# Four key heads of one batch per round: K and V each in one DMA of 128 rows, V's gradient first

## The chip, the core and the metric

The kernel runs on one core of a Trainium2 chip. The metric is the device time of one execution in microseconds (us). Three timed executions of the kernel before took 770.71, 771.0 and 772.86 us; the median, 771.0 us, is the time before. One further execution was profiled. It took 770.8 us, of which the profile's span covers 769.0 us. A core has five engines that run their own instruction streams: TensorE (PE), VectorE (DVE), ScalarE (ACT), GpSimd (POOL) and SyncE (SP). SP, ACT and POOL issue the DMAs, and every DMA runs on the same 16 DMA engines.

## What is computed

The kernel computes one decode step of a block and its gradients. A normalised input `xn` (2 batches, 512 features) goes through two branches: sliding-window attention against a cache, and a small dense layer with squared ReLU. The output is `x + s * silu(dense)`. The part that matters here is the attention branch and its gradients:

```
W = 4096                                   # the window: the last 4096 of 32768 positions
q = (xn @ wq) as 32 heads of 128           # 4 query heads share one of 8 key heads
p = softmax(q . k / sqrt(128))             # k, v: [2 batches, 8 heads, 4096, 128] of the window
o = p @ v ;  s = o @ wo
# gradients, for each batch and key head:
dv = p^T do                                # do: gradient that arrives at o
dp = do . v ;  ds = p * (dp - sum(dp * p))
dk = ds^T q ;  dq = ds k
```

The gradients of the K and V caches are returned whole: `out_2` and `out_3`, each [2, 8, 32768, 128] in bf16. Only the window of 4096 positions has values; the 28672 positions before it are zero in every head and have to be written.

## The kernel before, in words

**The zero fill.** Lines 91 to 114: POOL writes the zero positions of `out_2` and `out_3` from a tile of zeros `zt`, one head after the other, as 47 DMAs that are all issued from POOL's queue in order; each waits until an earlier one has landed, so that a limited number is under way. The very last head's zeros are written by SP at the end (line 626), after SP's store of `out_6`, and only when the second to last of POOL's fills has landed.

**The prologue** (lines 193 to 325). SP loads `w1`, `w2`, `wo` and `wq` (lines 203 to 207). Layer norm, the dense layer, `do` (lines 274 to 292) and `q` (294 to 304) are computed, and `w1` and `w2` are transposed for later (306 to 325). Its tiles live in a pool that is closed at its end, and the tiles `knat` and `vnat` for K and V are allocated after it in the same memory (lines 342 and 343), so the first loads of K and V wait for the prologue's end.

**A round** (lines 417 to 499) handles two key heads of both batches, that is four pairs of head and batch; there are four rounds. The window of one pair, 4096 x 128 bf16 values or 1 MB, is contiguous in memory; it is seen as 32 rows of 128 positions, 32 KB each. Pair number `pr` goes to the partitions `pr, pr+4, pr+8, ...` of a 128-partition tile by a DMA of 32 rows of its own (lines 345 to 347), so K of a round comes in four DMAs, and V too. Because of this interleaving the transposes use a permuted identity `pperm` (line 181), and `p_bf` and `ds_bf` are written with a stride of four elements (lines 440 and 452). The order inside a round is:

1. `scores(s_ps, knat, zq)` (lines 368 to 381): transpose K in 16 groups of eight blocks on PE, copy each group out of PSUM by DVE or ACT, multiply with the queries.
2. Softmax, and `p_bf` on ACT (line 440).
3. `scores(dp_ps, vnat, zdo)`, then `ds_bf` on DVE (line 452).
4. `contract(ds_bf, knat)` for dq (lines 383 to 399); then `outer_store` (401 to 412) makes the gradient of K: 32 matrix products (line 407), each evicted from PSUM by ACT or DVE into `knat` itself, and four DMAs of 1 MB from ACT's queue into `out_2` (line 412). Then SP loads K of the next round into `knat`, each quarter as soon as the store of that quarter has landed.
5. The same for V: `contract(p_bf, vnat)` for o, `outer_store` into `vnat`, four stores into `out_3`, four loads of the next V.
6. For the round's two heads the gradient of `wq` (lines 473 to 499), which overwrites `wq` in place.

The compiler's scheduler moves instructions of these steps past each other where their data allow it: the transposes of V, for instance, begin between those of K.

**The epilogue** (lines 501 to 633) takes tiles in the memory that `knat` and `vnat` give up, so it begins when the last stores have landed. It makes the output, the remaining gradients, the last zero fill on SP (626) and the store of `wo`'s gradient (633).

Of the kernel before, what the change touches and what calls it, by code (L numbers as in the profile page):

```python
# [16 lines left out]
def kernel(  # L17
# [36 lines left out]
    G = 8  # L54
    HH = 2
    NP = HH * B
    PB = P // NP
# [78 lines left out]
    doT_all = const.tile([P, HQ, B], BF16, name="doT_all")  # L136
    oT_all = const.tile([P, HQ, B], BF16, name="oT_all")
    dxqT = const.tile([P, DK, B], F32, name="dxqT")

# [40 lines left out]
    nc.vector.tensor_scalar(out=nsel[:], in0=sel[:], scalar1=1e30, scalar2=-1e30, op0=ALU.mult, op1=ALU.add)  # L180
    pperm = const.tile([P, NP, PB], BF16, name="pperm")
    nc.vector.tensor_copy(out=pperm[:], in_=ident_bf[:].rearrange("p (k b) -> p b k", b=NP))
    ZO = R - REP
# [3 lines left out]
    nc.vector.memset(zdo[:], 0.0)  # L187
    p_bf = const.tile([R, CC, PB, NP], BF16, name="p_bf")
    nc.vector.memset(p_bf[:], 0.0)
    ds_bf = const.tile([R, CC, PB, NP], BF16, name="ds_bf")  # L190
    nc.vector.memset(ds_bf[:], 0.0)

    with tc.tile_pool(name="pw", bufs=1) as pw:
# [7 lines left out]
        dma_store.dma_start(out=b2_bf[:], in_=B_b2.rearrange("(p k) -> p k", k=DK))  # L201
        w1 = pw.tile([P, DK, F], BF16, name="w1")
        dma_load.dma_start(out=w1[:], in_=B_w1.rearrange("(p k) f -> p k f", k=DK))
        w2 = pw.tile([P, FK, D], BF16, name="w2")
        dma_load.dma_start(out=w2[:], in_=B_w2.rearrange("(p j) d -> p j d", j=FK))
        dma_load.dma_start(out=wo[:], in_=A_wo.rearrange("(p j) m -> p j m", j=NJ))
        dma_load.dma_start(out=wq[:], in_=A_wq.rearrange("(p k) n -> p k n", k=DK))

        tp = ps_m.tile([P, DK, B], BF16, tag="m")
# [63 lines left out]

        do_rows = pw.tile([B, N], BF16, name="do_rows")
        JG = 4
# [17 lines left out]

        q_rows = pw.tile([B, N], BF16, name="q_rows")
        for n0 in range(0, N, 512):
# [30 lines left out]

    attn = ExitStack()
    kvp = attn.enter_context(tc.tile_pool(name="kvp", bufs=1))
    kvt = attn.enter_context(tc.tile_pool(name="kvt", bufs=3))
    wsl = attn.enter_context(tc.tile_pool(name="wsl", bufs=1))  # L330
    small = attn.enter_context(tc.tile_pool(name="small", bufs=1))
    one = attn.enter_context(tc.tile_pool(name="one", bufs=1))

    kwin = slice(SK - W, SK)

    def rows_of(t, b, h):
        return t[b, h, kwin, :].rearrange("(p c) d -> p c d", c=NCB)

    def pairs(r):
        return [(hh * B + b, b, r * HH + hh) for hh in range(HH) for b in range(B)]  # L340

    knat = kvp.tile([P, NCB, DH], BF16, name="knat")
    vnat = kvp.tile([P, NCB, DH], BF16, name="vnat")

    def load(src, r, nat):
        for pr, b, h in pairs(r):
            dma_load.dma_start(out=nat[pr:P:NP], in_=rows_of(src, b, h))

# [6 lines left out]
    def block_diag(hT):  # L355
        zr = small.tile([P, HH, B, G, REP], BF16, tag="zr")
        for hh in range(HH):
            for b in range(B):
                nc.vector.tensor_copy(out=zr[:, hh, b],
                                      in_=hT[:, hh * REP:(hh + 1) * REP, b].unsqueeze(1).to_broadcast([P, G, REP]))  # L360
        rp = ps_m.tile([R, P], F32, tag="m")
        nc.tensor.matmul(rp[:], lhsT=zr[:].rearrange("p h b g i -> p (h b g i)"), rhs=ident_bf[:, :], start=True, stop=True)
        bd = one.tile([R, G, DH], BF16, tag="bd")
        nc.vector.tensor_tensor(out=bd[:], in0=rp[:].unsqueeze(1).to_broadcast([R, G, DH]),  # L364
                                in1=m8[:].unsqueeze(2).to_broadcast([R, G, DH]), op=ALU.mult)
        return bd

    def scores(out_ps, nat, zbuf):
        n = 0
        for half in range(NH):  # L370
            for g in range(G):
                tp = ps_t.tile([P, CH, P], BF16, tag="pt")
                for j in range(CH):
                    nc.tensor.transpose(tp[:, j, :], nat[:, g * CC + half * CH + j, :], pperm[:].rearrange("p b k -> p (b k)"))  # L374
                tT = kvt.tile([P, CH, NP, PB], BF16, tag="tT")
                evac(tT[:].rearrange("p c b k -> p (c b k)"), tp[:].rearrange("p c k -> p (c k)"), eng=("act" if n % 4 == 3 else "dve"))
                n += 1
                for pr in range(NP):
                    o = ZO - (pr * RB + REP * g)
                    nc.tensor.matmul(out_ps[:, half * CH * PB:(half + 1) * CH * PB], lhsT=zbuf[:, pr, o:o + R], rhs=tT[:, :, pr, :],  # L380
                                     start=(g == 0 and pr == 0), stop=(g == G - 1 and pr == NP - 1))

    def contract(src, nat):
        cols = []
        for half in range(NH):
            tp = ps_t.tile([P, CH, R], BF16, tag="pt")
            for cc in range(CH):
                nc.tensor.transpose(tp[:, cc, :], src[:, half * CH + cc].rearrange("r k b -> r (k b)"), ident_bf[:, :])
            t = one.tile([P, CH, NP, G, REP], BF16, tag=f"colT{half}")
# [11 lines left out]
    def outer_store(src, bd, nat, dst, r):  # L401
        st = nat[:].rearrange("p (g c) d -> p g c d", g=G)
        n = 0
        for cc in range(CC):
            for gh in range(2):
                ov = ps_o.tile([P, 4, DH], F32, tag="o")
                nc.tensor.matmul(ov[:], lhsT=src[:, cc].rearrange("r k b -> r (k b)"), rhs=bd[:, gh * 4:(gh + 1) * 4, :],  # L407
                                 start=True, stop=True)
                evac(st[:, gh * 4:(gh + 1) * 4, cc, :], ov[:], eng=("act" if n % 8 in (0, 1, 3, 4, 6) else "dve"))
                n += 1  # L410
        for pr, b, h in pairs(r):
            dma_store.dma_start(out=rows_of(dst, b, h), in_=nat[pr:P:NP])

    NR = HKV // HH
    load(A_k_cache, 0, knat)
    load(A_v_cache, 0, vnat)
    for r in range(NR):
        hs = slice(r * HH * REP, (r + 1) * HH * REP)
        for hh in range(HH):
            hq = slice((r * HH + hh) * REP, (r * HH + hh + 1) * REP)  # L420
            nc.vector.tensor_copy(out=zq[:, hh * B:(hh + 1) * B, ZO:ZO + REP], in_=qT_all[:, hq, :].rearrange("p i b -> p b i"))
            nc.vector.tensor_copy(out=zdo[:, hh * B:(hh + 1) * B, ZO:ZO + REP], in_=doT_all[:, hq, :].rearrange("p i b -> p b i"))

        s_ps = ps_s.tile([R, CW], F32, tag="sd")
        scores(s_ps, knat, zq)
# [12 lines left out]
        for pr in range(NP):  # L438
            rb = slice(pr * RB, (pr + 1) * RB)
            nc.scalar.activation(out=p_bf[rb, :, :, pr], in_=e_sb[rb], func=ACT.Copy, scale=rl[rb, 0:1])  # L440

        dp_ps = ps_s.tile([R, CW], F32, tag="sd")
        scores(dp_ps, vnat, zdo)
        dpp = small.tile([R, 1], F32, tag="dpp")
# [5 lines left out]
        for pr in range(NP):  # L450
            rb = slice(pr * RB, (pr + 1) * RB)
            nc.vector.scalar_tensor_tensor(out=ds_bf[rb, :, :, pr], in0=dp_c[rb], scalar=delta[rb, 0:1], in1=p_bf[rb, :, :, pr],  # L452
                                           op0=ALU.subtract, op1=ALU.mult)

        dq_ps = contract(ds_bf, knat)
        dqT_bf = small.tile([P, HH, REP, B], BF16, tag="dqT_bf")
        for hh in range(HH):
            nc.scalar.mul(out=dqT_bf[:, hh].rearrange("p i b -> p b i"), in_=dq_ps[:, hh * B:(hh + 1) * B, :], mul=SCALE)
        bdq = block_diag(qT_all[:, hs, :])
        outer_store(ds_bf, bdq, knat, out_2, r)  # L460
        if r + 1 < NR:
            load(A_k_cache, r + 1, knat)

        o_ps = contract(p_bf, vnat)
        for hh in range(HH):
            hq = slice((r * HH + hh) * REP, (r * HH + hh + 1) * REP)
            nc.vector.tensor_copy(out=oT_all[:, hq, :].rearrange("p i b -> p b i"), in_=o_ps[:, hh * B:(hh + 1) * B, :])
        bddo = block_diag(doT_all[:, hs, :])
        outer_store(p_bf, bddo, vnat, out_3, r)
        if r + 1 < NR:  # L470
            load(A_v_cache, r + 1, vnat)

        for hh in range(HH):
            hk = r * HH + hh
            wqT = wsl.tile([P, REP, DK, P], BF16, tag="wqT")
# [8 lines left out]
            for k in range(DK):  # L484
                for i in range(REP):
                    nc.tensor.matmul(xps[:, k, :], lhsT=wqT[:, i, k, :], rhs=dqT_bf[:, hh, i, :], start=(i == 0), stop=(i == REP - 1))
            if hk == 0:
# [4 lines left out]
            for i in range(REP):  # L492
                nc.tensor.transpose(tp[:, i, :], dqT_bf[:, hh, i, :], ident_bf[:, :])
            dq_rows = small.tile([B, REP * DH], BF16, tag="dq_rows")
# [166 lines left out]
```

## Time and profile before

| What | Value |
|---|---|
| Median of three timed runs | 771.0 us |
| The profiled execution: time, span | 770.8 us, 769.0 us |
| Busy share of the span: PE, DVE, ACT, POOL | 53%, 36%, 28%, 4% |
| Bytes moved by DMA | 326.73 MB, mean 425 GB/s |
| of them read from and written to memory | 45.62 MB, 280.50 MB |
| One load of K or V: a DMA of 1024 KB, issue to landing | 14.8 us and 14.7 us (medians) |
| One store of 1024 KB, K and V | 28.0 us and 31.0 us (medians) |
| One zero fill of 7168 KB | 162.9 us (median, several under way) |

How to read it: the time of an execution is a little longer than the span, since the span runs from the first to the last recorded instruction. The profile's second part cuts the span into 40 slices of 19.2 us and gives, for each, the busy share of every engine in tenths, the clock granted to PE, the mean busy share of the 16 DMA engines and their bandwidth. The third part lists the DMA queues: q0 is POOL's, q1 SP's, q10 ACT's; its columns are the number of packets, the MB, and the time of the packets as a share of the time of all 16 DMA engines. The chain of waits follows the work that ended last back to its beginning; each of its lines is a start, a duration and what took it.

### The profile page before, as it was taken

How to read it: one execution, taken by the hardware profiler on the slowest of the kernel's cores; microseconds unless marked ns; L12 is line 12 of the kernel's file. 1: busy time of each engine (PE TensorE's matmuls, PEld its weight loads, DVE VectorE, ACT ScalarE, POOL GpSimd, SP SyncE). 2: the span in 40 equal slices, each digit the busy share in tenths (PEclk: the TensorE clock that was granted, in tenths of full speed). 3: DMA queues.
4: the chain of work that ended last, by engine and by line, in shares of the span. 5: the costliest groups of instructions: out<-in, count | busy, mean ns of one | idle time of the engine just before them, and what ended most of it. 6: DMA issues, size and time to landing. Idle time of an engine off the chain costs nothing.

```text
span 769.0 us, 9484 instructions
## 1 busy us (share of the span) xinstructions
PE 407.4 (53%) x4110; PEld 273.6 (36%) x4118; DVE 279.2 (36%) x496; ACT 213.9 (28%) x317; POOL 31.9 (4%) x55
## 2 busy tenths in 40 slices
PE   0166740875870656578034649702746784075690
PEld 0153330755520545442034447201635541034220
DVE  3033330435650232555012355610324463014770
ACT  0034430240660114066001315700231273010360
POOL 3000000010100000000000000000000000000000
PEclk9997895986975788688569687955978696565555
DMA  9999999999999999999999999999999999999988
GB/s 360 427 432 426 434 434 431 425 428 434 430 432 426 430 431 432 431 432 428 433 432 429 433 432 427 430 432 432 430 433 427 427 432 430 431 439 423 394 374 373
DMA packets 14971, 326.73 MB, mean 425 GB/s; under 512 B 3109, under 2 KB 3118, under 8 KB 3128
## 3 DMA queue, kind: packets, MB, share of 16 engines
q0 software_dynamic: 9728, 227.55, 70.1%
q1 hardware_dynamic: 3082, 56.63, 18.0%
q10 hardware_dynamic: 2120, 41.95, 12.9%
q8 instruction: 32, 0.52, 0.2%
q14 instruction: 9, 0.07, 0.0%
HBM read 45.62 MB, written 280.50 MB: 424 GB/s over the span
## 4 chain that ended last, share of the span: by engine, by line
DMA 41%; PE 31%; DVE 12%; ACT 9%; issue 4%; ACTq 1%; SPq 0%; DVEq 0%
DMA out_dram<-vnat 16%; DMA out_dram<-knat 13%; DMA vnat<-in_A_v_cache_dram 8%; PE dp_ps L380 5%; DMA b_bf<-in_B_b_dram 4%; PE ov L407 4%; PE tp L374 4%; PE ps L396 3%; DVE ds_bf L452 3%; ACT p_bf L440 2%; ACT tT L147 2%; PE wps L631 2%; DVE tT L149 2%; ACT knat L147 2%; PE dops L286 1%
## 5 line engine op out<-in xcount | busy, mean ns | idle before, releaser
L149 DVE COPY tT<-tp 128x1024 bf16<-128x1024 bf16 x96 | 64.3, 689 | 245.4 <-PE tp L374 245.4
L374 PE MATMUL tp<-pperm,knat 128*128 128x128 bf16 x512 | 42.2, 234 | 112.5 <-DMA knat<-in_A_k_cache_dram 85.6
L147 ACT COPY tT<-tp 128x1024 bf16<-128x1024 bf16 x32 | 32.4, 1012 | 181.3 <-PE tp L374 181.2
L374 PEld LDWEIGHTS <-knat 128*128 128x128 bf16 x512 | 37.0, 106 | 120.0 <-issue 118.3
L380 PE MATMUL dp_ps<-tT,zdo 128*128 128x256 bf16 x256 | 44.8, 314 | 31.1 <-ACT tT L147 24.1
L374 PE MATMUL tp<-pperm,vnat 128*128 128x128 bf16 x512 | 45.9, 246 | 25.8 <-DMA vnat<-in_A_v_cache_dram 23.4
L97 POOL DMA_DIRECT2D out_dram<-zt x47 | 30.8, 661 | 531.5 <-DMA out_dram<-zt 528.3
L407 PE MATMUL ov<-bd,p_bf 128*128 128x512 bf16 x124 | 44.3, 416 | 13.1 <-DVE bd L364 6.8
L374 PEld LDWEIGHTS <-vnat 128*128 128x128 bf16 x512 | 40.6, 113 | 29.3 <-issue 26.6
L147 ACT CAST knat<-ov 128x512 bf16<-128x512 f32 x80 | 43.9, 590 | 23.5 <-PE ov L407 20.2
L147 ACT CAST vnat<-ov 128x512 bf16<-128x512 f32 x80 | 43.5, 593 | 21.8 <-PE ov L407 10.7
L407 PE MATMUL ov<-bd,ds_bf 128*128 128x512 bf16 x124 | 45.5, 413 | 1.9 <-issue 0.9
L380 PE MATMUL s_ps<-tT,zq 128*128 128x256 bf16 x256 | 40.9, 293 | 10.4 <-DVE tT L149 6.2
L380 PEld LDWEIGHTS <-zdo 128*128 128x128 bf16 x256 | 27.5, 110 | 40.4 <-issue 35.2
L149 DVE CAST knat<-ov 128x512 bf16<-128x512 f32 x48 | 32.9, 691 | 23.5 <-PE ov L407 14.1
L149 DVE CAST vnat<-ov 128x512 bf16<-128x512 f32 x48 | 33.0, 692 | 21.9 <-PE ov L407 21.3
L380 PEld LDWEIGHTS <-zq 128*128 128x128 bf16 x256 | 25.8, 104 | 16.9 <-issue 13.6
L396 PEld LDWEIGHTS <-vnat 128*128 128x128 bf16 x512 | 20.1, 99 | 17.7 <-issue 12.2
L147 ACT CAST wq<-wps 128x512 bf16<-128x512 f32 x16 | 8.7, 591 | 59.0 <-DMA out_dram<-knat 54.9
L440 ACT ACTIVATE p_bf<-e_sb,rl 32x512 bf16<-32x512 f32 x16 | 22.8, 1428 | 6.7 <-DVE rl L437 6.5
L396 PE MATMUL ps<-t,vnat 128*128 128x16 bf16 x512 | 21.5, 171 | 5.9 <-issue 5.8
L407 PEld LDWEIGHTS <-p_bf 128*128 128x128 bf16 x128 | 12.0, 101 | 32.2 <-issue 28.3
(204 smaller groups left out, 526.8 us busy)
## 6 DMA issues: line engine op xcount, KB each, us to landing
out_dram<-zt POOLq DMA_DIRECT2D x26, 7168.0 KB, 162.9
knat<-in_A_k_cache_dram SPq DMA_DIRECT2D x16, 1024.0 KB, 14.8
vnat<-in_A_v_cache_dram SPq DMA_DIRECT2D x16, 1024.0 KB, 14.7
out_dram<-knat ACTq DMA_DIRECT2D x16, 1024.0 KB, 28.0
out_dram<-vnat ACTq DMA_DIRECT2D x16, 1024.0 KB, 31.0
out_dram<-zt POOLq DMA_DIRECT2D x4, 3584.0 KB, 56.6
out_dram<-zt SPq DMA_DIRECT2D x1, 7168.0 KB, 30.9
out_dram<-zt POOLq DMA_DIRECT2D x1, 5040.0 KB, 73.7
```

The lines of the kernel that those rows point to most:

```text
L97: sw_fill.append(nc.gpsimd.dma_start(out=v, in_=zs))
L147: nc.scalar.copy(out=out_ap, in_=in_ap)
L149: nc.vector.tensor_copy(out=out_ap, in_=in_ap)
L286: nc.tensor.matmul(dops[0:B, :, :], lhsT=dsT_bf[:, dk, :], rhs=woT[:, :, dk, :], start=(dk == 0), stop=(dk == DK - 1))
L374: nc.tensor.transpose(tp[:, j, :], nat[:, g * CC + half * CH + j, :], pperm[:].rearrange("p b k -> p (b k)"))
L380: nc.tensor.matmul(out_ps[:, half * CH * PB:(half + 1) * CH * PB], lhsT=zbuf[:, pr, o:o + R], rhs=tT[:, :, pr, :], start=(g == 0 and pr == ...
L396: nc.tensor.matmul(ps[:], lhsT=nat[:, g * CC + half * CH + cc, :], rhs=cols[half][:, cc, :, g, :], start=(half == 0 and g == 0 and cc == 0 ...
L407: nc.tensor.matmul(ov[:], lhsT=src[:, cc].rearrange("r k b -> r (k b)"), rhs=bd[:, gh * 4:(gh + 1) * 4, :], start=True, stop=True)
L440: nc.scalar.activation(out=p_bf[rb, :, :, pr], in_=e_sb[rb], func=ACT.Copy, scale=rl[rb, 0:1])
L452: nc.vector.scalar_tensor_tensor(out=ds_bf[rb, :, :, pr], in0=dp_c[rb], scalar=delta[rb, 0:1], in1=p_bf[rb, :, :, pr], op0=ALU.subtract, o ...
L631: nc.tensor.matmul(wps[:], lhsT=o_rows[:, j:N:NJ], rhs=ds_rows[:, :], start=True, stop=True)
```

## The change

A round now handles four key heads of one batch (the rounds are heads 0 to 3 of batch 0, then of batch 1, then heads 4 to 7 of each). The four heads' windows are 32 rows of 32 KB each, and one DMA carries all 128 rows, head `h` to the partitions `32h` to `32h+31`: one load per round for K and one for V, and one store for each. In memory a head's 32 rows are contiguous, and the next head begins 32768 positions further on, so the memory side of this DMA has the dimensions 4 heads x 32 rows x 16384 elements, and the tile's side 128 x 16384. With that layout the plain identity takes the place of `pperm`, and `p_bf` and `ds_bf` are written without a stride.

The order in a round changes: scores with V first, then scores with K, softmax, `p_bf`; then o and V's gradient, its store and the next V load; then dq and K's gradient, its store and the next K load. The first V is loaded in the prologue, behind `wq` in SP's queue, into memory of its own; `w1` and `w2` lie in K's tile, so K's first load still waits until they have been transposed. `do_rows` and `q_rows` share memory. dq is kept for both batches, and the gradient of `wq` is computed in the second round of each set of heads, for four heads at a time. The zero fill, its DMAs and its order are unchanged.

```diff
-    HH = 2
-    NP = HH * B
+    NP = 4
...
-    pperm = const.tile([P, NP, PB], BF16, name="pperm")
-    p_bf = const.tile([R, CC, PB, NP], BF16, name="p_bf")
+    p_bf = const.tile([R, CC, NP, PB], BF16, name="p_bf")
...
+    w12 = kvp.tile([P, NCB * DH], BF16, tag="k")
+    w1 = w12[:, 0:DK * F].rearrange("p (k f) -> p k f", k=DK)
+    w2 = w12[:, DK * F:DK * F + FK * D].rearrange("p (j d) -> p j d", j=FK)
+    rounds = [(b, h0) for h0 in range(0, HKV, NP) for b in range(B)]
+
+    def kv_of(t, r):
+        b, h0 = rounds[r]
+        return t[b, h0:h0 + NP, SK - W:SK, :].rearrange("h (k c) d -> h k (c d)", c=NCB)
+
+    def load(src, r, tag):
+        nat = kvp.tile([P, NCB * DH], BF16, tag=tag)
+        dma_load.dma_start(out=nat[:], in_=kv_of(src, r))
+        return nat[:].rearrange("p (c d) -> p c d", d=DH)
...
         dma_load.dma_start(out=wq[:], in_=A_wq.rearrange("(p k) n -> p k n", k=DK))
+        vnat = load(A_v_cache, 0, "v")
...
-    def load(src, r, nat):
-        for pr, b, h in pairs(r):
-            dma_load.dma_start(out=nat[pr:P:NP], in_=rows_of(src, b, h))
...
-        for pr, b, h in pairs(r):
-            dma_store.dma_start(out=rows_of(dst, b, h), in_=nat[pr:P:NP])
+        dma_store.dma_start(out=kv_of(dst, r), in_=nat.rearrange("p c d -> p (c d)"))
...
+    knat = load(A_k_cache, 0, "k")
     for r in range(NR):
...
+        dp_ps = ps_s.tile([R, CW], F32, tag="sd")
+        scores(dp_ps, vnat, zdo)
         s_ps = ps_s.tile([R, CW], F32, tag="sd")
         scores(s_ps, knat, zq)
...
+        bddo = block_diag(heads(doT_all, r))
+        o_ps = contract(p_bf, vnat)
...
+        outer_store(p_bf, bddo, vnat, out_3, r)
+        if r + 1 < NR:
+            vnat = load(A_v_cache, r + 1, "v")
+
+        bdq = block_diag(heads(qT_all, r))
         dq_ps = contract(ds_bf, knat)
...
         outer_store(ds_bf, bdq, knat, out_2, r)
         if r + 1 < NR:
-            load(A_k_cache, r + 1, knat)
...
+            knat = load(A_k_cache, r + 1, "k")
+
+        b, h0 = rounds[r]
+        for hk in range(h0, h0 + NP) if b == B - 1 else ():
```

## Prediction

> **What bounds the kernel now.** I read the slices first, for which resource is full; then the queue table, for what fills it; then the chain of waits in order of time, for what a round of K and V costs.
>
> The slices, their DMA rows:
>
> ```profile
> DMA  9999999999999999999999999999999999999988
> GB/s 360 427 432 426 434 434 431 425 428 434 430 432 426 430 431 432 431 432 428 433 432 429 433 432 427 430 432 432 430 433 427 427 432 430 431 439 423 394 374 373
> ```
>
> All 16 DMA engines are full from the first slice to the last. 326.73 MB at the middle's 431 GB/s are 758 us of the span's 769; the rest is the start and the end. The kernel is bound by bytes, and the change moves not one byte less. It can win only in the lulls, and lose by leaving engines idle.
>
> The queue table (packets, MB, share of 16 engines):
>
> ```profile
> q0 software_dynamic: 9728, 227.55, 70.1%
> q1 hardware_dynamic: 3082, 56.63, 18.0%
> q10 hardware_dynamic: 2120, 41.95, 12.9%
> ```
>
> Two readings. First, the speed of one engine: q10 moved 41.95 MB in 12.9% of 16 x 769.0 us = 1587 engine-us, so 26.4 GB/s per engine; q0 gives the same 26.4. Second, how many engines a DMA is dealt to. q10 carried 32 stores of 32 rows, two of 128 rows (`wq`, `wo`), two small loads of 128 rows and two of 2 rows: 1024+256+256+4 = 1540 rows. That leaves 580 packets: 16 for each of the 36 DMAs of 32 or 128 rows (576), and 2 for each of the two with 2 rows (4). q1 agrees: 2437 data packets, and 645 = 40 DMAs x 16, two 2-row DMAs x 2 and a 1-row DMA x 1. So each engine of a DMA leaves one small packet, and a DMA's first dimension decides the number of engines: 16 for 32 or 128 rows, two for 2 rows, one for 1.
>
> The chain of one round (start, us, what):
>
> ```profile
> 380.34 31.85 DMA out_dram<-vnat
> 412.20 12.36 DMA vnat<-in_A_v_cache_dram
> 424.69 1.01 PE tp L374 x8
> ...
> 485.47 33.10 DMA out_dram<-knat
> ```
>
> V arrives at 424.6, K's store goes out at 485, both stores and the last quarter of the V load take 77 us more, and V arrives again at 561.8: 137 us per round, hidden under the fill. The last fill follows at 735.0, behind the epilogue.
>
> **The DMA shape, on which all turns.** The new DMA's memory side has the dimensions 4 x 32 x 16384 (the heads are 32768 positions apart and cannot be merged with the rows), its tile side 128 x 16384. In the trace both sides of every DMA have the same first dimension, so it does not show which side rules. The rows bound it: 16 engines, if 128 rules, or 4, if the smaller does. I take 4: the pieces must be cut alike on both sides, and 16 shares of a first dimension of 4 do not exist, as they did not for 2 rows and for 1. That the four are the same ones each time I take too, and price the other case below.
>
> [...]
>
> **Part 1, the four engines' load.** K and V move 16 x 4.19 MB = 67.1 MB; on four engines that is 16.8 MB each. The fill puts 227.55/16 = 14.2 MB on each, the rest (326.73-227.55-67.1 = 32.1 MB) 2.0. Together 33.0 MB, at 26.4 GB/s **1250 us** for these four; the twelve others have 16.2 MB, 615 us. So even with no idle moment the span is 1250, as an end of the range.
>
> **Part 2, the chain on top of it.** One K or V transfer, alone on four engines: 4.19 MB / (4 x 26.4 GB/s) = 39.7 us. Beside others it gets these shares:
> - load beside fill, window 20 to 50: q1 54.9%, so 39.7/0.55 = 72 us
> - store beside fill, window 645 to 672: q10 46.0%, so 86 us
> - store, load and fill, window 385 to 410: 29.5%, 31.5%, 41.2%, so about 130 us for store and load together.
>
> First K arrival: `wq` landed at 57; V behind it takes 72 (129); K, which is issued at 108 when `w1` and `w2` are transposed, follows in SP's queue with another 72: **201**. V was there at 129, so its scores (20 us) are done.
>
> From K's arrival to V's store: scores with K 20 us (395.3 to 415.6 before, 15 of 16 groups), softmax and `p_bf` 10 (426.5 to 436.5), transposes of `p_bf` and contraction 7 (461.6 to 467, with DVE's copy), 32 products with their evictions 16 (468.9 to 485): **53 us**. Then V's store 86; under it `ds_bf` (5.4 us), the dq contraction (5.4) and K's product and evictions (16), 27 in all, are hidden. K's store, behind V's in ACT's queue, runs beside the next V load: 130. Then K's load, under which V's scores are hidden: 72. A round is 53+86+130+72 = **341 us**.
>
> How long the fill lasts on the four engines: it needs 14.2 MB/26.4 = 539 us of each. Until 201 it got about 85 (201, less 8 of start, less 29 for `w1`, `w2`, `wo`, `wq`, less 79 for V and K); each round gives it 341 - 4 x 39.7 = 182. So it has 267 at 542, 449 at 883, and ends in the third round, near 1006. From there transfers run undisturbed: in that round V's store ends at 1015, K's store and V's load share the engines (79, to 1094), K's load 39.7, to 1134. Last round: 53, V's store 39.7, K's store 39.7: 1266. The epilogue then takes what it took before, from 674.7 to 735.0, 60 us, and the last fill and `wo`'s store 34 (735.0 to 769.0): a span of **1360 us**, and with the 1.8 us around it 1361.8. The profiled execution (770.8) stands 0.2 us under the median, so I take 1362.
>
> **Smaller parts.**
> - 48 fewer issues and their packets: SP's four K issues took 2.45 us, ACT's four stores 2.41. All are beside full DMA engines; between windows with few and many small packets (275 to 340 and 245 to 275) the bandwidth differs by 431 to 426 GB/s. Zero taken, at most 1% of the K/V stretches gained.
> - The staged quarters go: SP's next load used to start after one quarter of the store (four issues spread over 21.9 us) and now waits for all of it. Behind it in SP's queue is only the next K load, which waits for a later store. Priced in the round above, which has no overlap of a store with its own load.
> - `p_bf` and `ds_bf` without stride: L440 took 1.43 us on ACT, L452 1.34 on DVE. Below, the nearest row is the 128x512 eviction, 0.59 (ACT) and 0.69 (DVE); above, no change. A gain of 0 to 3.4 us per round for `p_bf`; `ds_bf` hides under V's store. I take the nearest row, L440 itself, zero. That a stride gone makes it slower, I exclude: same elements, same engine. `ident_bf` for `pperm`: the same 128x128 product, zero.
> - PE's clock: granted 0.79 in the window 425 to 485; longer pauses might raise it, or not. If all 53 us shrank by 0.79, 11 us per round, 44 in all, to the lower side.
> - V in the prologue: a loss of DMA time to nobody, since the prologue waits for small loads of `b1`, which land before (33.7).
> - The gradient of `wq`, four heads in the last round where there were two: 16 evictions of 0.59 or 0.69 and 8 copies of `wqT` of 0.68 or 1.03 us, some 17 us, under K's last store of 39.7. Without that cover, 17 us more.
> - Shared memory of `do_rows` and `q_rows`: the transposes of `do_rows` ended at 90.0, the first `q_rows` products at 88.3; up to 1.7 us, hidden as K's load waits for V's.
>
> **The rivals.**
> 1. *Sixteen engines (128 rules)*, which ends on the other side. Place: the stores and loads. A transfer then takes a quarter: 18 us for a load, 21 for a store, 32 for both; a round 53+21+32+18 = 124 instead of 137, K arrives at 126, the last store ends at 126+372+53+21+10 = 582 instead of 674.7. For it: every 128-row DMA here ran on 16. Price: bytes stay the bound, so only the lull before the last fill closes (window 727 to 736: 2.27 MB where 431 GB/s give 3.88, 3.7 us): 767. It decides whenever the dealing gives 16 engines: then there is no loss to pay for. If the lull stays because the fill's last DMAs still end first, 771.
> 2. *Four engines, but different ones each time.* Against it, nothing in the trace. The engines' loads even out, the fill ends near 740; rounds cost 53+86+80+72 = 291 beside it (K's store and V's load apart) and 53+3 x 39.7 = 172 after it: 201+2 x 291+172+53+79+60+34, about 1181.
> 3. *Fill starved or favoured.* In the 4-engine case with other shares: a fill that gets less early leaves less idle later, down to 1250 and the start's 8, 1258; one that runs out a round earlier leaves them idle for 53 us more, 1415, and with the `wq` work uncovered 1432.
>
> **How the numbers follow.** Four fixed engines 0.79, four changing 0.06, sixteen 0.13 (0.09 at 767, 0.04 at 771), other 0.02, which I count as slower. The likeliest is 1362; its own range, 1258 to 1432, takes in clock, `p_bf` and shares. The other 4-engine case brings the lower end to 1180; that leaves out the sixteen and a little, 2 in 10. A measurement of this kernel can tell some 0.3% from no change. Faster 0.09, same 0.04, slower 0.87.
>
> **What would show it.** The small packets: with four engines q1 falls to 3082-512+32 = 2602 packets and q10 to 1640; with sixteen to 2698 and 1736. The DMA row drops to fives and sixes, about 240 GB/s; a 4096 KB load lands after 70 us or more instead of some 18; `ds_bf` and K's evictions end under V's store; DMA takes over half of the chain. What would make me wrong: q1 at 2698, and the DMA row still at nines.

## The result and the profile after

The changed kernel takes 1500.3 us (median of four runs, 1493.4 to 1501.7), against 770.9 us for the kernel before on the same chip: a ratio of 1.943, with a 95% interval from 1.937 to 1.950. The prediction had the direction and the cause, four DMA engines, but its 1362 us was 138 too low, and the time lies outside its range (1180 to 1432). The profiled execution took 1501.7 us, its span 1499.8.

The DMA rows of the slices, now 37.5 us each:

```profile
DMA  9993659926747989755436657522222220122308
GB/s 395 419 399 129 229 211 428 372 95 254 292 175 329 411 340 427 312 238 235 195 155 248 244 222 316 223 93 108 104 109 99 93 69 2 41 67 85 144 35 372
```

The nines are gone. In the six slices from 975 to 1200 us the busy share stands at two tenths: 4 of 16 engines is 25%, and four times 26.4 GB/s is 106. That is the plateau of 93 to 109 GB/s. The 34th slice (from 1237 us) with 2 GB/s is the last round's computing, in which hardly any DMA runs.

The queue table, same columns as before:

```profile
q0 software_dynamic: 9728, 227.55, 36.0%
q1 hardware_dynamic: 2602, 56.63, 10.0%
q10 hardware_dynamic: 1640, 41.95, 8.1%
```

Two things are to be seen. The packet counts are 2602 and 1640, to the packet what the prediction gave for four engines (sixteen would have been 2698 and 1736). And the speed of an engine has fallen: q10 moved its 41.95 MB in 8.1% of 16 x 1499.8 us = 1944 engine-us, 21.6 GB/s; before, the same bytes took 1587, at 26.4. This second reading is where the miss lies, as the experiments show.

The chain of waits, by engine, and its two longest pieces of the first round:

```profile
another core or an unknown queue 61%; PE 23%; DVE 7%; ACT 4%; DMA 2%; issue 2%; ACTq 0%; DVEq 0%
```

```profile
269.25 209.96 another core or an unknown queue
...
501.00 59.24 another core or an unknown queue
```

The first line looks like a puzzle: one core alone runs here. For the DMAs of K and V this profile gives no time to landing, which is probably why the chain names no queue. What the pieces are is said by the list of waits on PE:

```profile
PE tp L368 <- DMA nat<-in_A_v_cache_dram: 615.7, 4, 210.0
PE tp L368 <- DMA nat<-in_A_k_cache_dram: 209.9, 4, 59.3
```

PE waits 826 us in eight waits for V and K. In the 210 us lie the rest of V's store (V's load is issued behind it, at 349.6), then K's store and V's load beside each other (K's load is issued behind K's store, at 473.5, and V is there at 479).

### The profile page after: what moved, and what is told of

It reads as the page before. It is cut to its first block, busy times and chain, and to the rows that moved or that the text cites. A ratio compares the mean times of both kernels' runs of the same rounds, so it can differ in the third digit from the quotient of the medians.

```text
span 1499.8 us, 9389 instructions
## 1 busy us (share of the span) xinstructions
PE 414.4 (28%) x4110; PEld 272.5 (18%) x4118; DVE 267.4 (18%) x483; ACT 203.2 (14%) x313; POOL 31.9 (2%) x55
## 3 DMA queue, kind: packets, MB, share of 16 engines
q1 hardware_dynamic: 2602, 56.63, 10.0%
q10 hardware_dynamic: 1640, 41.95, 8.1%
## 4 chain that ended last, share of the span: by engine, by line
another core or an unknown queue 61%; PE 23%; DVE 7%; ACT 4%; DMA 2%; issue 2%; ACTq 0%; DVEq 0%
PE ov L401 4%; PE tp L368 3%; PE dp_ps L374 3%; PE s_ps L374 2%; DMA b_bf<-in_B_b_dram 2%; DVE tT L149 2%; PE ps L390 2%; ACT nat L147 1%; DVE nat L149 1%; ACT tT L147 1%; PE wps L619 1%; PE tp L382 1%; PE dops L299 1%; PE sps L506 1%
## 5 line engine op out<-in xcount | busy, mean ns | idle before, releaser
L368 PE MATMUL tp<-ident_bf,nat 128*128 128x128 bf16 x1024 | 89.1, 241 | 827.2 <-DMA nat<-in_A_v_cache_dram 615.7
L368 PEld LDWEIGHTS <-nat 128*128 128x128 bf16 x1024 | 77.8, 110 | 834.9 <-DMA nat<-in_A_v_cache_dram 617.7
L147 ACT CAST nat<-ov 128x512 bf16<-128x512 f32 x160 | 87.6, 589 | 45.2 <-PE ps L390 24.9
L149 DVE CAST nat<-ov 128x512 bf16<-128x512 f32 x96 | 65.4, 690 | 52.4 <-PE ov L401 51.3
L486 PE MATMUL wps<-dq_rows,xn_bf 2*128 2x512 bf16 x32 | 14.0, 506 | 92.8 <-ACT wq L147 87.5
L374 PEld LDWEIGHTS <-zdo 128*128 128x128 bf16 x256 | 26.4, 107 | 22.9 <-issue 18.9
L390 PE MATMUL ps<-t,nat 128*128 128x16 bf16 x1024 | 28.2, 173 | 7.8 <-DVE bd L358 7.8
L390 PEld LDWEIGHTS <-nat 128*128 128x128 bf16 x1024 | 28.2, 103 | 11.0 <-issue 5.8
L374 PEld LDWEIGHTS <-zq 128*128 128x128 bf16 x256 | 25.6, 103 | 19.6 <-issue 16.5
L149 DVE CAST wq<-wps 128x512 bf16<-128x512 f32 x16 | 11.0, 690 | 100.7 <-PE wps L486 100.2
L401 PEld LDWEIGHTS <-ds_bf 128*128 128x128 bf16 x128 | 13.4, 111 | 23.2 <-issue 20.9
L147 ACT CAST dw_st<-wps 128x512 bf16<-128x512 f32 x15 | 8.8, 585 | 47.8 <-PE wps L599 45.0
L469 PE MATMUL tp<-ident_bf,wq 128*128 128x128 bf16 x128 | 14.9, 224 | 0.1
```

The lines of the kernel that those rows point to most:

```text
L147: nc.scalar.copy(out=out_ap, in_=in_ap)
L149: nc.vector.tensor_copy(out=out_ap, in_=in_ap)
L390: nc.tensor.matmul(ps[:], lhsT=nat[:, g * CC + half * CH + cc, :], rhs=cols[half][:, cc, :, g, :], start=(half == 0 and g == 0 and cc == 0 ...
L401: nc.tensor.matmul(ov[:], lhsT=src[:, cc].rearrange("r b k -> r (b k)"), rhs=bd[:, gh * 4:(gh + 1) * 4, :], start=True, stop=True)
L469: nc.tensor.transpose(tp[:, jj, :], wq[:, k, n0:n0 + DH], ident_bf[:, :])
```

## The experiments

**First: which of the changes costs the time?** Theory 1 is the prediction's: the memory side's first dimension of 4 deals each DMA to the same four engines. The rivals are the size of the DMA, and the new order.

*One DMA per head.* The changed kernel, with four DMAs of 32 rows per transfer.

```diff
-        dma_load.dma_start(out=nat[:], in_=kv_of(src, r))
+        for h in range(NP):
+            dma_load.dma_start(out=nat[h * PB:(h + 1) * PB], in_=kv_of(src, r)[h])
...
-        dma_store.dma_start(out=kv_of(dst, r), in_=nat.rearrange("p c d -> p (c d)"))
+        for h in range(NP):
+            dma_store.dma_start(out=kv_of(dst, r)[h], in_=nat[h * PB:(h + 1) * PB].rearrange("p c d -> p (c d)"))
```

> The changed kernel, but K and V of a round in four DMAs each, one per head, of 32 rows to 32 neighbouring partitions: the first dimension is 32 on both sides, everything else stays. Theory 1 (the memory side's first dimension of 4 deals the DMA to the same four engines): 16 engines again, the DMA rows at nines, q1 back at 3082 packets and q10 at 2120, and about 767 us, as the prediction's rival of sixteen engines had it (765 to 775). Theory 2 (a DMA of 4 MB in one issue is slow, whatever its dimensions): also about 767. Theory 3 (the new order, V first, or the late loads cost the time): still above 1400 us.

Measured: 829.1 us, 1.077 of the kernel before (1.072 to 1.083). Theory 3 falls: the order is the changed kernel's, and 671 us of its time are gone. But 767 was expected. All sixteen engines work, with the packet counts of before, and yet:

```profile
DMA  9999999999999999999999999999999999999996
GB/s 361 429 400 335 430 368 307 430 429 434 313 370 370 350 431 431 431 411 403 394 369 384 435 426 430 364 388 353 365 432 432 430 426 385 387 433 428 421 434 289
...
q1 hardware_dynamic: 3082, 56.63, 21.3%
q10 hardware_dynamic: 2120, 41.95, 14.0%
```

The busy share is nine tenths in all slices but the last, but the bandwidth falls to 307 to 400 GB/s in many of those in which K and V move. Engines can be busy and slow. q1 needed 21.3% of 16 x 825.1 us, 2812 engine-us, where it had needed 2215; q10 1848 instead of 1587. The excess of 858, over 16 engines, is 54 of the 56 us by which the spans differ (825.1 and 769.0).

*Rows first.* Still one DMA of 128 rows per transfer, with the two outer dimensions of the memory side exchanged. Row r of head h then lies at partition 4r+h, so `pperm` and the strided `p_bf` and `ds_bf` of the kernel before return.

```diff
-        return t[b, h0:h0 + NP, SK - W:SK, :].rearrange("h (k c) d -> h k (c d)", c=NCB)
+        return t[b, h0:h0 + NP, SK - W:SK, :].rearrange("h (k c) d -> k h (c d)", c=NCB)
```

> The changed kernel, with K and V of a round still in one DMA of 128 rows each, but with the 32 rows as the memory side's first dimension and the four heads as its second (row r of head h to partition 4r+h, so the permuted identity and the strided p_bf and ds_bf come back). Theory 1 (first dimension): 32 and 128 are both dealt to 16 engines, q1 2698 and q10 1736 packets, about 767 us, up to 24 us of the softmax's strided writes hidden under the fill. Theory 2 (size): about 1500 us, as the changed kernel.

Measured: 769.2 us in ten runs (768.9 to 769.5), 0.9951 of the kernel before (0.9926 to 0.9976). Its rows:

```profile
GB/s 360 432 429 420 438 429 425 434 427 436 425 430 434 430 425 430 436 430 429 429 433 429 436 431 430 428 431 432 427 433 434 429 434 431 423 435 424 433 427 322
...
q1 hardware_dynamic: 2698, 56.63, 17.7%
q10 hardware_dynamic: 1736, 41.95, 12.9%
```

Same bytes, same 128 rows in one issue, same order: 731 us faster than the changed kernel by the order of two dimensions. Theory 2, the size, falls. The counts are the 2698 and 1736 of sixteen engines. The exchange also puts the heads on other partitions, which the second part takes up.

*Two heads per DMA.* As the first edit, with `h:h + 2` in place of `h`, so the memory side's first dimension is 2.

> The changed kernel, with K and V of a round in two DMAs of two heads each: the memory side's first dimension is 2. Theory 1 (same engines by the first dimension): two engines carry all of K and V, 67.1 MB / 2 / 26.4 GB/s = 1271 us each, with the fill's 539 and 76 for the rest 1886 us at least, and with idle time and slower packets as in the changed kernel (250 us over its 1250) 2050 to 2500 us; q1 2602 packets again (16 loads x 2). Theory 2 (size): 2 MB per DMA lies between 771 and 1500 us. Theory 4 (as many engines as the first dimension, but others each time): about 1500 us or less, since two DMAs would fill four engines.

Measured: 2336 us, in one run. Theory 4, others each time, falls. A stretch of loads, the fill having ended (window 1900 to 2000):

```profile
DMA  1111111111101111111111110110111111011000
GB/s 26 26 52 26 26 39 39 26 39 39 26 26 39 26 39 39 26 39 39 26 39 39 26 52 26 26 52 26 26 52 39 26 52 39 26 52 26 13 13 0
...
q1 hardware_dynamic: 105, 3.31, 11.8%
```

Two DMAs had been issued together, each on two engines, and 11.8% of 16 is 1.9 engines: the same two. Over the runs the memory side's first dimension of 4 gave four engines (2602 packets), 2 gave two (these lines) and 32 gave sixteen (2698). Which of the sixteen they are no run here shows, only that they are the same ones.

**Second: why are the packets slow?** In the kernel before a packet of 32 KB took 1.23 us (window 694.5 to 697: q10's 18 packets took 55.4% of 16 x 2.5 us). In the changed kernel's last stretch only its two last stores run (window 1320 to 1400):

```profile
q10 hardware_dynamic: 200, 6.36, 24.1%
```

24.1% of 16 x 80 us is 308 engine-us for 194 packets of 32 KB, 1.59 us each. Nothing else was moving. Before K's store joins it, V's store alone is slower still (window 1286 to 1307):

```profile
q10 hardware_dynamic: 36, 1.18, 25.3%
```

25.3% of 16 x 21 us is 85 engine-us for 36 packets, 2.36 us each. I took the four engines to be in each other's way: at the tile (theory P; if each carries one head, they work on the partitions i, 32+i, 64+i, 96+i) or in memory (theory M; their rows then lie 8 MB apart).

*Transfers alone.* A kernel that holds only these lines (the remarks at their ends are added here) and leaves out the computation, with a small write of DVE after each transfer that waits for its landing:

```diff
+    for rep in range(2):
+        far_store()          # (a) changed kernel's store
+        near_store()         # (b) groups of rows 1.03 MB apart in memory
+        far_store_blocks()   # (c) 4 heads x 8 rows from 32 neighbouring partitions, four DMAs
+        head_store()         # (d) one head per DMA, four DMAs
+        far_load()
+        near_load()
+        far_load_blocks()
```

> Transfers of 4.19 MB by themselves, each after the one before has landed, twice: (a) the changed kernel's store: 4 heads 8 MB apart x 32 rows of 32 KB, head h from partitions 32h to 32h+31; (b) the same partitions, the four groups of rows 1.03 MB apart in memory; (c) 8 MB apart again, but in four DMAs of 4 heads x 8 rows from 32 neighbouring partitions, so that the four engines' partitions lie 8 apart instead of 32; (d) four DMAs of one head, 32 rows; then loads in the shapes of (a), (b) and (c). Everything else of the computation is left out. At 26.4 GB/s per engine a transfer on four engines takes 39.7 us, on sixteen 10. In the changed kernel the last stores ran at 79 GB/s, 1.6 us per 32 KB packet instead of 1.23. Theory P (two engines that work 32 partitions apart get in each other's way at the tile): (a) and (b) slow, 50 to 80 us, (c) 40. Theory M (rows 8 MB apart get in each other's way in memory): (a) and (c) slow, (b) 40. If neither: all of them 40, and the slow packets come from the queue of two stores. (d) 10 to 14 us.

Measured, DVE's small writes in order of time; the bracket is the wait for the transfer:

```profile
79.13 0.06 DVE L58 MEMSET nat<- 128x4 uint32 x1 [69.74 <-DMA out_dram<-nat]
148.85 0.06 DVE L58 MEMSET nat<- 128x4 uint32 x1 [69.66 <-DMA out_dram<-nat]
190.04 0.06 DVE L58 MEMSET nat<- 128x4 uint32 x1 [41.13 <-DMA out_dram<-nat]
211.63 0.06 DVE L58 MEMSET nat<- 128x4 uint32 x1 [21.52 <-DMA out_dram<-nat]
286.01 0.06 DVE L58 MEMSET nat<- 128x4 uint32 x1 [74.32 <-DMA nat<-in_A_k_cache_dram]
363.84 0.06 DVE L58 MEMSET nat<- 128x4 uint32 x1 [77.76 <-DMA nat<-in_A_k_cache_dram]
405.49 0.06 DVE L58 MEMSET nat<- 128x4 uint32 x1 [41.59 <-DMA nat<-in_A_k_cache_dram]
```

(a) and (b) took the same 69.7 us: 8 MB or 1.03 MB apart in memory made no difference, theory M falls. (c), on four engines too, took 41, as theory P had it. (c) also has four DMAs in place of one; the next run has one DMA per transfer throughout. (d) is the form of the first experiment: sixteen engines, but 21.5 us where 10 to 14 were expected. If an engine takes its rows in one block, each has two neighbouring partitions there, and the next engine's lie two further on. That engines so close are in each other's way would fit the 54 us of the first experiment, but it is argued here, not shown.

*Two engines alone.* The same frame, with two engines and other distances between their partitions. (The profile does not say which engine carries which row; the distances are those of one block of rows for each engine.)

```diff
+            go(nat[0:64], 32)     # (a) 32 apart
+            go(nat[0:72], 36)     # (b) 36 apart
+            go(nat[0:P:2], 32)    # (c) 64 apart
+            go(nat[0:32], 16)     # (d) 16 apart
+            go(nat[0:2], 1)       # (e) 1 apart
```

> Transfers by themselves, with a first dimension of 2 on the memory side, each after the one before has landed; first stores, then loads, each list twice. The two engines' partitions lie (a) 32 apart, 32 rows each; (b) 36 apart, 36 rows each; (c) 64 apart, on every second partition, 32 rows each; (d) 16 apart, 16 rows each; (e) one row each, 1 apart. The rest of the computation is left out. Theory P in its narrow form (partitions 32 apart share a way into the tile in groups of four, those 36, 64 and 16 apart do not): (a) 2.4 us per packet, 70 us or more; (b) 1.21, 46 us; (c) 1.21, 41; (d) 1.21, 21; (e) 2.4, neighbours of one group. Theory N (any two engines alone are slow): all 2.4. Theory S (slow where the whole set spans more than 32 partitions): (a), (b) and (c) slow, (d) and (e) fast.

Measured, the first list of stores:

```profile
79.10 0.06 DVE L55 MEMSET nat<- 128x4 uint32 x1 [69.71 <-DMA out_dram<-nat]
125.18 0.06 DVE L55 MEMSET nat<- 128x4 uint32 x1 [46.02 <-DMA out_dram<-nat]
166.09 0.06 DVE L55 MEMSET nat<- 128x4 uint32 x1 [40.85 <-DMA out_dram<-nat]
187.69 0.06 DVE L55 MEMSET nat<- 128x4 uint32 x1 [21.55 <-DMA out_dram<-nat]
191.56 0.06 DVE L55 MEMSET nat<- 128x4 uint32 x1 [3.81 <-DMA out_dram<-nat]
```

(a) to (d) fall on the side that the narrow form gave them. 32 apart was slow (69.7 us for 32 packets in a row on each engine), 36 apart was not (46.0 for 36), though both sets span more than 32 partitions and both use two engines alone; theories N and S fall. (c) and (d), 32 and 16 packets on each engine, differ by 19.3 us: 1.21 per packet, which leaves about 2.2 us of a transfer as fixed. With that taken off, (a) is 67.5 us for its 32 packets, 2.1 per packet, a little under the 2.4. (e), one packet on each engine, is then 1.6, between the two rates: whether 1 apart is slow the times do not decide. The loads repeat (a) to (d), with 72.4, 46.4, 41.8 and 22.5 us; (e) took 4.4. What is measured is these distances; that partitions share a way into the tile, and in groups of four, was the theory's and is not shown.

*Eight apart.* The test of the miss itself: the changed kernel, still on four engines, with the partitions arranged so that by theory P the engines do not meet. Row 8j+q of head h goes to partition 32j+8h+q; loads wait for the whole store, as in the changed kernel.

```diff
-        dma_load.dma_start(out=nat[:], in_=kv_of(src, r))
+        for j in range(4):
+            ld = dma_load.dma_start(out=nat[32 * j:32 * j + 32], in_=kv_of(src, r)[:, 8 * j:8 * j + 8])
...
-        dma_store.dma_start(out=kv_of(dst, r), in_=nat.rearrange("p c d -> p (c d)"))
+        for j in range(4):
+            last_store[tag] = dma_store.dma_start(out=kv_of(dst, r)[:, 8 * j:8 * j + 8],
+                                                  in_=nat[32 * j:32 * j + 32].rearrange("p c d -> p (c d)"))
```

> The changed kernel, still with a first dimension of 4 on the memory side, but every transfer in four DMAs of 4 heads x 8 rows, each to or from 32 neighbouring partitions, so that the four engines work 8 partitions apart and not 32 (a load still waits for the whole store before it; the transposes use a permutation to match). Theory P (the miss of 138 us comes from packets that two engines 32 apart slow down for each other): four engines again, 24 or 25% DMA share where only K and V move, but packets at 1.23 us, a mean within 0.03 of it, and the span of the prediction's own sum, 1360 us, within 40. If the slow packets come from four engines alone, or from the shares beside the fill: about 1500 us again.

Measured: 1336.2 us in one run, a span of 1334.2, 26 from the prediction's 1360 and inside the 40. Its queues, and its last stores (window 1165 to 1235):

```profile
q1 hardware_dynamic: 2698, 56.63, 10.2%
q10 hardware_dynamic: 1736, 41.95, 7.4%
```

```profile
q10 hardware_dynamic: 260, 7.47, 24.7%
```

The same 24 to 25% of the engines, but 107 GB/s where the changed kernel had 79; q10's 41.95 MB took 7.4% of 16 x 1334.2 us, 1580 engine-us, 26.6 GB/s. (The counts are 2698 and 1736 because four DMAs on four engines leave as many small packets as one on sixteen.)

**Third: does the rest of the change gain anything?** The rows-first kernel was run again, beside the new order with the four interleaved DMAs of the kernel before (the lines below, on top of the rows-first edit).

```diff
+        for h in range(NP):
+            dma_load.dma_start(out=nat[h:P:NP], in_=kv_of(src, r)[:, h])
...
+        for h in range(NP):
+            dma_store.dma_start(out=kv_of(dst, r)[:, h], in_=nat[h:P:NP].rearrange("p c d -> p (c d)"))
```

> The kernel of the second experiment once more (one DMA of 128 rows, rows as the memory side's first dimension), beside the next one on the same chip. It took 0.9951 of the time before, with an interval from 0.9926 to 0.9976. If its gain is real: 768 to 770 us, 0.2 to 0.5% under the kernel before.

> The new order (V first, first V in the prologue, four heads of one batch) with the DMAs of the kernel before: four of 32 rows per transfer, head h to the partitions h, h+4, h+8 and so on. Theory G1 (the new order gives the small gain, since the chain ends earlier and the fill runs through to the end): as the one-DMA form, 768 to 770 us. Theory G2 (the 48 DMAs fewer, with their small packets, give it): 771, as before.

Measured: rows first 769.4 us (0.9945, from 0.9915 to 0.9976), the new order with four DMAs 770.3 us (0.9956, from 0.9921 to 0.9992). Both are faster than the kernel before by an interval that leaves out 1, so the order gives part of it (G1), and every run of the one-DMA form (769.1 to 769.7) is below every run of the four-DMA form (769.8 and up), so the 48 DMAs fewer give about 0.9 us more (G2). But the lowest times lie closer together: 770.2 before, 769.8 with four DMAs, 769.1 with one. The rest of G1's part is that the times of the kernel before reach further up. How much of the first part is the lull at the end and how much the start stays open. One DMA per transfer in the old order was not tried.

The four-DMA form also bears on the first experiment. Both have the new order, four DMAs of 32 rows per transfer and the packet counts of the kernel before; the partitions differ, neighbouring there, every fourth here (and with them the permuted identity and the strided writes): 829.1 and 770.3 us. With all sixteen engines at work, the choice of partitions made 59 us.

## Why the prediction was right and wrong

The four engines were right, and so was the sum's form; the spans can be laid beside it term by term. Times in us; the middle columns come from the issue times of the DMAs and PE's first transposes after each arrival.

| Term | Predicted | Changed kernel | Eight apart |
|---|---|---|---|
| First K arrives | 201 | 204 | 180 |
| K's arrival to V's store, four times | 212 | 188 | 186 |
| V's store beside the fill, three times | 251 | 287 | 243 |
| K's store with V's load, three times | 339 | 352 | 330 |
| K's load, three times | 184 | 255 | 217 |
| The last two stores | 79 | 117 | 80 |
| Epilogue and last fill | 94 | 98 | 99 |
| Span | 1360 | 1500 | 1334 |

- **Direction, engine count, the same engines each time: right**, each with its own experiment. The trace before, in which both sides of a DMA have the same first dimension, decided neither the four nor that they are the same; the 2602 and 1640 packets and the 1.9 engines of the two DMAs issued together did.
- **The step that failed is "One K or V transfer, alone on four engines: 4.19 MB / (4 x 26.4 GB/s) = 39.7 us".** Alone it took 69.7 us as a store and 74 to 78 as a load. I took an engine's speed from a kernel with another layout: the kernel before interleaves its four pairs (`nat[pr:P:NP]`), and nothing in its trace shows two engines meeting. The changed layout puts the four heads, and with one head on each the four engines, 32 partitions apart. In the engines' budget the excess over the eight-apart kernel is (1944 - 1580) + (2400 - 2177) = 587 engine-us in q10 and q1, 147 us for each of the four: with it Part 1's bound of 1250 is about 1397. With the engines eight apart, the last two stores took 79.7 us, the prediction's 79.4. In the kernel the loss is smaller than alone: 147 us over the 16 transfers is 9 us each, not 30, and the last two stores took 117 us, not twice 69.7. Why it is smaller when other packets are in the engines' queues was not tested. It is not shown either why the kernel before is free of the loss: if each engine took its rows in a block of two, some of its engines would have partitions 32 apart as well, and its packets still took 1.23 us.
- **The fill's end "near 1006" was wrong too.** The K-load row shows it: the prediction let the third round's load run undisturbed, 39.7, and it took 82.6. In the window 1050 to 1150 of the changed kernel the fill was still there:

```profile
q1 hardware_dynamic: 116, 3.80, 9.3%
q10 hardware_dynamic: 112, 3.60, 8.4%
q0 software_dynamic: 116, 3.15, 7.5%
```

116, 112 and 116 packets: the counts are as good as equal, as they would be if an engine took a packet from each of the three queues in turn; the order itself is not shown. The fill's share is then 28 KB of 92, 30%, not the 41.2% that I had read in the window 385 to 410 of the kernel before. Its lines show why that one was larger:

```profile
q0 software_dynamic: 155, 4.39, 41.2%
q1 hardware_dynamic: 157, 3.31, 31.5%
q10 hardware_dynamic: 152, 3.15, 29.5%
```

The counts are as good as equal there too, but 3.31 MB are only 101 rows of 32 KB: a third of K's and V's packets were the small ones that each DMA leaves, and each transfer was four DMAs. What this error cost by itself is not shown. In the eight-apart kernel the fill lasted past 1050 as well, and there the terms moved both ways: K's loads 33 us over the sum, the first K and the four stretches to V's store 47 under. That its span came within 26 us of the sum is in part luck.
- **The first K at 201 was hit by luck**: 204 with slow packets, but 180 with the engines eight apart.
- **53 us to V's store: right, 6 too high** in each round (47).
- **The rival of sixteen engines** gave 767; rows first took 769.2. But it said that any dealing to sixteen engines has no loss to pay for, and the kernel with one DMA per head, on sixteen engines, paid 58 us, which the argument at (d) above puts down to engines that meet.
- **The range** ended at 1432, from the fill's timing and the `wq` work (17 us, hidden). Its upper end had no term for a slower engine, though the 26.4 GB/s came from another layout.

## What to carry to other kernels

Read a DMA by its dimensions before its bytes: in these runs the memory side's outermost dimension set how many of the 16 engines work (two for 2, four for 4, sixteen for 32), and exchanging two dimensions was worth 731 us. Then ask which partitions the engines touch at the same moment, since a full busy share does not mean full speed: MB per engine-us from the queue table shows it at once (ACT's queue: 26.4 GB/s before, 21.6 in the changed kernel; SP's queue: 25.6 before, 20.1 with one DMA per head). A speed that is read from a trace holds for that trace's layout, and a change of layout is a reason to widen the range.

## What the runs showed of the hardware that was not expected

- Two DMA engines, with their blocks of rows 32 partitions apart, took 2.1 us for a 32 KB packet (69.7 us for 32 in a row on each); at 16, 36 and 64 apart it was 1.2 (21.6 us for 16, 46.0 for 36, 40.9 for 32).
- On four engines, rows 8 MB apart in memory were stored no slower than rows 1.03 MB apart (69.7 us both, and 41 us for the eight-apart form at 8 MB).
- Engines can count as busy while they move less: 9 tenths at 307 GB/s in the kernel with one DMA per head.
- Three queues on the same engines were served the same number of packets (116, 112 and 116 in 100 us), though the fill's were of 28 KB and the others of 32; so too beside the small ones (155, 157 and 152 in 25 us).
